# An adaLN-conditioned block: filling matmuls ahead of the first transposes, and another issue table

## The chip, the cores and the metric

The kernel runs on one core of a Trainium2 chip. Its engines work side by side, each through its own queue in strict order: TensorE (matmuls, PE in the profile), VectorE (DVE), ScalarE (ACT), GpSimd (POOL) and SyncE (SP), which issues most of the transfers between HBM and the on-chip memory. Matmul results land in PSUM, everything else lives in SBUF. The metric is the device time of one launch in microseconds. All inputs are bf16.

## The reference

```python
x = A_x                                            # 1 x 2048 x 512
sa, ca, ga, sb, cb, gb = split6(silu(c) @ w_mod)   # six rows of 512
h = layernorm(x) * (1 + ca) + sa
x = x + ga * A(h)
h = layernorm(x) * (1 + cb) + sb
x = x + gb * B(h)
```

`A` is an attention with 32 heads of 16 channels. A token looks at itself and at 7 earlier ones, two apart (window 8, dilation 2), with a softmax over these eight; `wqkv` (512 x 1536) goes in, `wo` (512 x 512) comes out. `B` normalises again, without scale and shift, and mixes over the tokens: `u = gelu(h^T @ w1 + b1)` with `w1` of 2048 x 1792, then `y = u @ w2 + b2` with `w2` of 1792 x 2048, transposed back.

## The kernel before

**Operations and the table.** The work is cut into 805 named operations. Each is added to a graph with what it reads and writes, the slot it takes or frees, and one or more ways to do it, each on another engine (`add`, `add_any`). A hand-written table, `ORDER`, names all of them once. `schedule()` walks it and issues each operation at its place; a mark behind the name picks the way: `:d` VectorE, `:a` ScalarE, `:p` POOL, `:s` nothing at all, `:q` a matmul in four pieces of 32 columns. Without a mark it is the first way. So the table fixes each engine's queue; what runs when follows from the waits between the queues. All engine instructions are issued through one wrapper, and so nearly every row of the profile has line 131: operations are told apart by tile and shape. Slots come from pools: six PSUM banks (psS), four large buffers (big), five vD buffers; a slot goes to the one that has been free longest.

**Tokens.** 2048 tokens are 16 tiles of 128 (`xx`, indices 0 to 15), in chunks of 2, 4, 4, 4 and 2 tiles. For each tile stand `ln1s`, `ln1v` (statistics, on VectorE, or on ScalarE as two passes into `junk`), for each chunk `rstd1`, `rste1`, `nb1` (inverse deviation and its product with the mean), and `n1` (normalise). Chunks 0 and 1 are transposed on TensorE (`tr0_0`, `tr1_0`, `tr1_2`), and the result is scaled by `a1col` as it is copied out (`hT0_k`, `hT1_k`); the later ones by DMA (`xt6` to `xt15`), with the scale multiplied into the weights (`wsc`).

**Modulation.** `cps` turns c into a column, `silu_exp` and `silu_dve` make silu(c), `modcols1` and `modcols0` multiply it with the first third of `w_mod` (loaded by `ld_wmod1`, `ld_wmod0`) in 16 one-column matmuls each. `a1col` is 1 + ca, `sab` is sa, from which `qvb0`, `qvb1` make the bias of q and v. The other four rows come later (`modrow`, `mrows`, `ld_row0` to `ld_row3`); the first is multiplied into `wo` (`woq_s`).

**Attention, chunk by chunk.** `qkv{ch}_{t}{j}` makes q (t=0), k (1) and v (2), `ev..` copies them out. `qk{ch}_0..3` multiplies q with eight shifted k on VectorE into a big buffer, `red` sums over channels on TensorE into `psL`. Then `max` (VectorE), `sub` (TensorE), `exp` (ScalarE), `esum` (TensorE), `rcp`, `rcq` (ScalarE), `smB` (VectorE); the weights and v are spread over partitions by DMA (`a2`, `vd`), `pv{ch}_0..3` multiplies them on VectorE, `pvacc` sums on TensorE, `oev` copies out, `wo{tile}` multiplies with woq, `x1_{tile}` writes the new x. After that `ln2..`, `n2`, `aff`, `afb`, `ln3..` and `h3` give the input of B.

**The MLP.** `mlp1_{i}_{ft}_{s}` adds token tiles from s on into the F-tile ft, in two or three passes over the tokens, whose parts are parked (`park`) and added (`padd`); then `gelu`. The slices of `w1` come through a ring of three buffers, wst0 to wst2 (`ld_w1_{i}_{f}`), which early on hold raw `wqkv`. `mlp2_{tile}` is the second product, `fin` the residual, `st_out` the store.

**Filling matmuls.** `WARM` is a list of eight counts. Block `warm0` (12 matmuls of 128 x 512, all of the identity with itself) is an operation of its own, tied in between `cps` and the `modcols` products by the key `wmA1`. The other seven may be done or skipped; the table skips six (`:s`) and has `warm1` (2 matmuls) as its last entry.

## Time and profile before

| what | us |
|---|---|
| median of three runs (lowest, highest) | 198.6 (197.77, 198.84) |
| span of the profiled execution | 196.8 |
| TensorE busy | 185.2 |
| VectorE busy | 156.6 |
| ScalarE busy | 124.9 |
| POOL busy | 19.9 |
| first transposes, `tr0_0`, start | 6.47 |
| `warm0`, start and length | 7.30, 5.20 |
| `modcols1`, start | 12.33 |
| first qkv product, start | 14.55 |
| first q·k product on VectorE, start | 18.07 |

The span runs from the first to the last instruction of one execution; the time of a run holds some 1.8 us more. Busy time is the time in which an engine has an instruction in it. Neighbouring matmuls overlap in the records, so the time from one start to the next says more about them than their own lengths. In a timeline row stand the start, the length, the engine, and behind the tiles how many instructions the row gathers; in brackets how long the engine was idle before it and what ended that.

### The profile page before, as it was taken

Reading aid. Unit: us, or ns where it says so; the run is one execution under the profiler, and the core shown is the slowest. Engines: PE = TensorE matmul, PEld = TensorE weight load, DVE = VectorE, ACT = ScalarE, POOL = GpSimd, SP = SyncE. Lnnn points to the kernel's source line nnn. Section 1 sums busy time; section 2 is a strip of 40 time slices with the busy share of each in tenths; the row PEclk is TensorE's granted clock in tenths of the full one; section 3 lists DMA queues with packets and bytes.
Section 4 is the critical chain, followed back from the end, with each engine's and each line's share of the span. In section 5 each row is a group of like instructions: output and inputs, shape, how many; then the busy total and the mean of one; then the engine's idle time right before and its main releaser. Section 6 shows DMA issues by size and latency. Waiting matters only on the chain.

```text
span 196.8 us, 4628 instructions
## 1 busy us (share of the span) xinstructions
PE 185.2 (94%) x1850; PEld 95.5 (48%) x1867; DVE 156.6 (80%) x244; ACT 124.9 (63%) x293; POOL 19.9 (10%) x38
## 2 busy tenths in 40 slices
PE   0699999999999999899999999999999999999994
PEld 0369554654444467244544454444444444444453
DVE  2888999999999999999999999965841633453664
ACT  6877999998999999999797889812760000000000
POOL 5123006320000005030000031200000000000000
PEclk9999999999999999999999999999999999999999
DMA  5998478778899732969674768888939293001112
GB/s 169 312 366 248 115 165 256 235 216 238 165 193 317 252 131 80 312 167 249 199 200 136 159 176 180 197 250 170 336 65 309 82 257 102 30 27 53 53 53 82
DMA packets 55369, 35.95 MB, mean 183 GB/s; under 512 B 24628, under 2 KB 52788, under 8 KB 55348
## 3 DMA queue, kind: packets, MB, share of 16 engines
q1 hardware_dynamic: 53468, 34.05, 63.2%
q10 hardware_dynamic: 1880, 1.61, 2.5%
q8 instruction: 14, 0.23, 0.5%
q14 instruction: 7, 0.06, 0.1%
HBM read 22.03 MB, written 2.10 MB: 123 GB/s over the span
## 4 chain that ended last, share of the span: by engine, by line
PE 73%; DVE 13%; ACT 5%; issue 3%; DMA 2%; SPq 1%; POOL 0%; DVEq 0%; ACTq 0%
PE psS L131 71%; DVE big L131 9%; DVE h L131 2%; PE psL L131 2%; ACT junk L131 1%; SPq L131 1%; DMA vD<-v_sb 1%; ACT xx L131 1%; DMA xx<-in_A_x_dram 1%; DVE m L131 1%; ACT o_sb L131 1%; ACT lsb L131 0%; DVE mv L131 0%; POOL h L131 0%; ACT v_sb L131 0%
## 5 line engine op out<-in xcount | busy, mean ns | idle before, releaser
L131 PEld LDWEIGHTS <-wst 128*128 128x128 bf16 (+1 forms) x566 | 35.5, 100 | 31.9 <-issue 1.3
L131 PE MATMUL psS<-h,wst 128*32 128x512 bf16 (+1 forms) x400 | 50.5, 379 | 0.4 <-issue 0.3
L131 DVE TENSOR_TENSOR big<-q_sb,k_f 128x4096 bf16<-128x4096 bf16 (+1 forms) x20 | 36.4, 1857 | 0.5 <-ACT k_f L131 0.5
L131 DVE TENSOR_TENSOR big<-a2sb,vD 128x4096 bf16<-128x4096 bf16 (+1 forms) x20 | 36.6, 1858 | 0.0
L131 DVE SCALAR_TENSOR_TENSOR h<-psS,bcol,rows_bc 128x512 f32<-128x512 f32 (+2 forms) x18 | 12.4, 690 | 24.2 <-PE psS L131 24.0
L131 PE MATMUL psS<-hT,w_qkv 128*32 128x512 bf16 (+3 forms) x414 | 28.7, 337 | 0.8 <-ACT v_sb L131 0.4
L131 PEld LDWEIGHTS <-w_qkv 128*32 128x32 bf16 (+1 forms) x462 | 19.9, 108 | 16.4 <-issue 2.7
L131 PE MATMUL psS<-gT,big 128*128 128x512 bf16 x109 | 24.3, 379 | 0.2
L131 POOL TENSOR_SCALAR h<-xx,rs,nb 128x512 bf16<-128x512 bf16 x6 | 10.6, 1777 | 84.2 <-DVE nb L131 84.2
L131 PEld LDWEIGHTS <-big 128*128 128x128 bf16 x144 | 12.0, 98 | 13.7 <-issue 0.5
L131 ACT ACTIVATE junk<-xx 128x512 bf16<-128x512 bf16 x28 | 17.7, 631 | 1.3 <-DVE xx L131 0.3
L131 ACT ACTIVATE h<-xx,nb,rs 128x512 bf16<-128x512 bf16 x22 | 17.2, 818 | 0.4 <-DVE nb L131 0.4
L131 PE MATMUL psS<-woq,o_sb 128*32 128x512 bf16 (+1 forms) x123 | 15.8, 380 | 0.4 <-ACT o_sb L131 0.4
L131 ACT ACTIVATE gT<-psS,bcol 128x512 bf16<-128x512 f32 x14 | 8.8, 686 | 10.6 <-DVE psS L131 10.6
L131 DVE TENSOR_TENSOR psS<-psS,gT 128x512 f32<-128x512 f32 x14 | 9.2, 695 | 6.3 <-PE psS L131 6.3
L131 DVE TENSOR_TENSOR h<-h,xx 128x512 bf16<-128x512 f32 (+2 forms) x18 | 11.4, 633 | 0.7
L131 ACT ACTIVATE q_sb<-psS,qvb 128x512 bf16<-128x512 f32 (+1 forms) x20 | 11.6, 603 | 0.3 <-PE psS L131 0.2
L131 PEld LDWEIGHTS <-group 128*32 128x32 bf16 x288 | 7.0, 96 | 9.8 <-issue 4.0
L131 PE MATMUL psS<-hT,wst 128*128 128x256 bf16 (+2 forms) x74 | 11.3, 333 | 0.1
L131 ACT ACTIVATE v_sb<-psS,qvb 128x512 bf16<-128x512 f32 (+1 forms) x20 | 11.2, 607 | 0.0
L131 DVE TENSOR_TENSOR h<-h,rows_bc 128x1024 bf16<-128x1024 bf16 (+2 forms) x14 | 10.5, 759 | 0.0
L131 ACT ACTIVATE k_f<-psS 128x512 bf16<-128x512 f32 x16 | 9.7, 606 | 1.1 <-PE psS L131 1.1
(90 smaller groups left out, 223.3 us busy)
## 6 DMA issues: line engine op xcount, KB each, us to landing
vD<-v_sb SPq DMA_DIRECT2D x12, 524.5 KB, 4.8
big<-in_B_w_dram SPq DMA_DIRECT2D x4, 896.0 KB, 7.5
vD<-v_sb SPq DMA_DIRECT2D x8, 268.5 KB, 3.1
wst<-in_B_w_dram SPq DMA_DIRECT2D x3, 640.0 KB, 5.4
xx<-in_A_x_dram SPq DMA_DIRECT2D x7, 256.0 KB, 5.6
wst<-in_B_w_dram SPq DMA_DIRECT2D x2, 800.0 KB, 4.7
gT<-in_w_mod_dram SPq DMA_DIRECT2D x3, 512.0 KB, 5.4
wst<-in_B_w_dram SPq DMA_DIRECT2D x2, 768.0 KB, 5.6
```

The costliest lines, as they stand in the source:

```text
L131: r = fn(*a, **k)
```

## The change

`warm0` becomes a block like the others: it may be placed anywhere, and the `modcols` products no longer depend on it. The counts become (5, 1, 5, 2, 2, 2, 1, 2). A second list, `GATE`, gives each block a token tile or none. A block with a tile multiplies the identity with that tile of `xx` instead of with itself, and so waits for that tile's load: `warm2` tile 1, `warm3` tile 8, `warm4` tile 2, `warm5` tile 4, `warm6` tile 6. Nobody reads what the fills write.

`ORDER` is another table with the same 805 names. All eight blocks, 20 matmuls, now stand ahead of `tr0_0`: `warm7`, `cps`, `warm1`, `warm0`, `warm4`, `warm3`, `warm5`, `warm6`, `warm2`. Behind `tr0_0` come `modcols1`, `tr1_2`, `tr1_0`, `modcols0`, `qkv0_00`, `qvb0`, `qkv0_10`, `qkv0_02`, `qkv0_12` (before: `warm0`, `modcols1`, `modcols0`, `tr1_2`, `tr1_0`, `qvb0`, `qkv0_00`, `qkv0_02`, `qkv0_10`, `qkv0_12`). Some 75 operations are done in another way: `n1_0` on ScalarE and `n1_1` on POOL instead of the other way round, more of `wsc` and of the normalisations on POOL, `x1_10` on VectorE (which spares `wo10` the matmul that adds the old x). Fewer products are cut in quarters: 1867 matmuls become 1737. Everywhere else too the operations stand in another order: `smB0` behind `rcq0` with `ev0_20` and `ev1_12` ahead of them on ScalarE, `woq_s` ahead of `qkv2_11`, `ld_w1_0_1152` and the loads behind it at other places.

```diff
@@ -178,60 +178,60 @@
 ORDER = """
-halo0 ident ld_c act_table cps silu_exp ld_x1 ld_x0 ln1s0 ln1v0 ln1s1:a ln1v1 rstd1_0 rste1_0 ld_x_2_8 ld_x_1_2 nb1_0
-consts ln1s9 silu_dve n1_1 n1_0:p tr0_0 ln1s8 ld_x_1_4 ln1s4:a ld_x_2_6 ln1s3:a warm0 ln1s5 ln1s7 ld_wmod1 ln1v5
-ld_wmod0 modcols1 modcols0 ln1v9 ln1v8 ln1v4 ln1s2 ln1v2 ld_wqkv0 ln1v7 ln1v3 ln1s6 ln1v6 rstd1_1 rste1_1 nb1_1 n1_4:d
-rstd1_2 rste1_2 n1_2:d n1_5:d nb1_2 ld_wqkv1 n1_3 n1_7 n1_6:d a1col hT0_2:d n1_9 tr1_2 tr1_0 hT1_1 wsc0_1:p hT0_1:d
-sab hT0_0:d ld_x_3_12 hT0_3:d hT1_3:d qvb0 qvb_cp0 qkv0_00 warm6:s wsc1_3:a hT1_2:d qkv0_02 ev0_00 ld_wqkv2 qkv0_10
-qkv0_12 ld_b2 ev0_10 ld_x_4_14 wsc1_2:p qkv0_20 wsc0_0 qvb1 ld_x_3_10 wsc0_3:p hT1_0:d ev0_02 wsc2_2:a ln1s13 ln1s12
-ev0_12 ln1v12 ln1v13 wsc1_1:a qkv0_22 qk0_1 qkv1_13 ld_wmod2 ld_wo3 qk0_0 qk0_2 n1_8 red0_0 red0_1 ln1s11:a qkv1_03:q
-qvb_cp1 qk0_3 xt6 red0_2 ld_wmod3 ev1_13 ev1_03 red0_3 mask wsc2_3:a ln1v11 ln1s10 ld_b1 ld_wo0 xt8 ev0_20 xt7 qkv1_11
-...
-n1_14 xt13 xt12 ln2q0 ln2q1 n1_15 qkv2_21 red2_1 red2_2 ln2w0 red2_3 xt11 rstd2_0 pv1_1 ev2_21 rste2_0 qkv3_10:q
-ev3_10 qkv3_02:q ev3_02 qkv3_00:q ev2_20 ev3_00 nb2_0 n2_1 n2_0 qkv3_11 max2 qkv3_01 ev3_01 sub2 pvacc1_1 oev1_1
-halo_v2 ld_row2 vd1_0 pvacc1_3 pv1_2 qkv3_12:q ld_row1 exp2 aff0 ev3_12 qkv3_13:q halo_v3:a ev3_11 pv1_0 esum2
-...
-fin6_0 mlp2_10_0 fin9_0 fin8_0 st_out8_0:a st_out6_0:a fin10_0 mlp2_7_0 fin7_0 st_out7_0:a mlp2_11_0 fin11_0 fin12_0
-st_out10_0:a st_out11_0:a st_out9_0 mlp2_14_0 fin14_0 st_out14_0 mlp2_13_0 fin13_0 st_out13_0:a mlp2_15_0 st_out12_0:a
-fin15_0 st_out15_0 mlp2_15_2 mlp2_15_1 fin15_2 fin15_1 st_out15_1 st_out15_2:a warm1
+ld_c ident warm7 act_table cps halo0 silu_exp silu_dve ld_x1 ln1s1 warm1 ln1v1 ld_x0 warm0 ld_x_2_8 ld_x_1_2 ln1s9:a
+ln1s0 consts warm4 ln1v0 rstd1_0 ln1s8 ld_x_1_4 ln1s3 ln1s5 ln1s2 ln1v9 warm3 ld_x_2_6 warm5 ln1v5 ln1v3 ln1v8
+ld_wmod1 ln1v2 rste1_0 ln1s4:a ln1v4 rstd1_1 rste1_1 warm6 nb1_0 ld_wmod0 n1_1:p warm2 ln1s7 n1_0 nb1_1 n1_4:p ln1s6
+n1_3:d n1_2:d ln1v7 ln1v6 tr0_0 rstd1_2 rste1_2 ld_wqkv0 n1_5:d modcols1 tr1_2 tr1_0 a1col ld_wqkv1 wsc1_0:p modcols0
+ld_x_3_12 hT0_2 nb1_2 hT0_0:d n1_6:d hT0_3:d hT1_2:d wsc0_1 hT0_1 sab hT1_3 ld_wqkv2 qkv0_00 ld_b2 wsc1_2:p wsc0_3:a
+hT1_0:d wsc0_2:a qvb0 ld_x_4_14 n1_8:d wsc0_0:a qvb_cp0 n1_7:d qkv0_10 ln1s13 ld_x_3_10 qkv0_02 ev0_00 ld_wmod2 ln1s12
+ev0_10 qkv0_12 hT1_1 qk0_1 ev0_02 qkv0_20 qk0_0 ld_wo3 ev0_12 ln1s15:a qkv0_22 qkv1_03 qkv1_13 red0_0 n1_9 ev1_03
+ln1v13 red0_1 qk0_2 ev1_13 qk0_3 red0_2 xt6 qkv1_11:q red0_3 mask qkv1_01 qvb1 ln1s10:a ln1s11 qk1_3 wsc1_1:a ev1_11
+...
+qkv2_02:q rcq1 ev2_11 ev2_01 oev0_2 pvacc0_1 oev0_0 nb1_4 n1_15:p ev2_02 smB1 qk2_1 xt10 ev2_13 red2_0 biascols
+qkv2_12 n1_14 vd1_3 qkv2_23 ev2_12 wo0 wo1 vd1_2 qk2_3 x1_0 ln2q0 x1_1 halo_v2 qkv2_20 xt11 qkv2_22 a2_1_0 biascols_cp
+qkv2_21 qk2_2 red2_1 a2_1_1 a2_1_2 a2_1_3 ev2_22 ln2m0 red2_2 ev2_20 ln2q1 xt13 xt12 pv1_2 ln2w0 red2_3 rstd2_0 ev2_23
+vd1_0 xt14 qkv3_00:q vd1_1 ld_row1 ev2_21 rste2_0 pv1_3 qkv3_12:q nb2_0 xt15 max2 pvacc1_2 qkv3_02 ev3_12 qkv3_01
+pv1_0 ld_row3 ev3_00 sub2 qkv3_10 oev1_2 n2_0 ev3_01 qkv3_03 n2_1 ev3_10 exp2 aff0 pvacc1_0 qkv3_11:q ev3_03 oev1_0
+pv1_1 ev3_11 esum2:q rcp2 halo_v3:a vd2_0 ev3_02 pvacc1_3 oev1_3 vd2_2 qkv3_20:q vd2_1 ev3_20 pvacc1_1 qkv3_13 qk3_0
+afb0 rcq2 smB2 a2_2_1 qkv3_23 oev1_1 ev3_13 wo3 wo5 ln3s1:a qk3_1 qk3_2 ev3_23 ln3s0:a x1_5 qkv3_22 x1_3 wo2 x1_2
+ln2q3 qk3_3 a2_2_0 wo4 x1_4 qkv4_00 ln2q4 red3_0 red3_1 qkv4_12:q a2_2_3 vd2_3 ln2q5 ln2q2 ev4_12 ln2m2 ev3_22 red3_2
+...
+mlp2_8_0 fin8_0 st_out5_0:a mlp2_10_0 st_out11_0:a st_out8_0:a st_out6_0 mlp2_14_0 fin9_0 st_out9_0:a mlp2_13_0
+fin10_0 st_out10_0:a fin14_0 st_out14_0:a mlp2_12_0 fin13_0 fin12_0 mlp2_15_0 st_out13_0 st_out12_0:a fin15_0
+mlp2_15_2 fin15_2 st_out15_0:a st_out15_2:a mlp2_15_1 fin15_1 st_out15_1:a
 """
@@ -264,7 +264,8 @@
     GRP=(2, 4, 4, 2, 1),
     XDMA=(2, 3, 4),
     INJ=(),
-    WARM=(12, 2, 2, 2, 2, 2, 2, 2),
+    WARM=(5, 1, 5, 2, 2, 2, 1, 2),
+    GATE=(None, None, 1, 8, 2, 4, 6, None),
 ):
     nc = _OrderedNC(tc, 1)
     G = _Graph(dict(ps=6, big=NBIG, vd=NVD))
@@ -522,20 +523,18 @@
 
     for w_, n_w in enumerate(WARM):
         s_w = _Slot("ps")
-
-        def f_warm(s_w=s_w, n_w=n_w):
+        g_w = GATE[w_]
+
+        def f_warm(s_w=s_w, n_w=n_w, g_w=g_w):
+            rhs = _ap(ident[:, 0:1], [[0, 4], [1, P]]) if g_w is None else xx[:, g_w, :]
             for _ in range(n_w):
-                nc.tensor.matmul(ps(s_w), lhsT=ident[:], rhs=_ap(ident[:, 0:1], [[0, 4], [1, P]]), start=True, stop=True)
-        if w_ == 0:
-            f_warm0, s_w0 = f_warm, s_w
-            continue
-        G.add_any([("pe", 0.216 * n_w, f_warm), ("skip", 0.0, lambda: None)], reads=["ident"], alloc=s_w, frees=s_w,
-                  name=f"warm{w_}")
+                nc.tensor.matmul(ps(s_w), lhsT=ident[:], rhs=rhs, start=True, stop=True)
+        G.add_any([("pe", 0.216 * n_w, f_warm), ("skip", 0.0, lambda: None)],
+                  reads=["ident"] + ([] if g_w is None else [("xx", g_w)]), alloc=s_w, frees=s_w, name=f"warm{w_}")
 
     s_c, s_m = _Slot("ps"), (_Slot("ps"), _Slot("ps"))
     add("pe", 0.18, lambda: nc.tensor.matmul(ps(s_c)[:, 0:KT], lhsT=c_t[:], rhs=ident[0:KT, 0:KT], start=True,
                                              stop=True), reads=["c_t", "ident"], alloc=s_c, name="cps")
-    add("pe", 0.216 * WARM[0], f_warm0, after=[G.ops[-1]], alloc=s_w0, frees=s_w0, writes=["wmA1"], name="warm0")
     add("act", 0.2, lambda: nc.scalar.activation(ecol[:], ps(s_c)[:, 0:KT], ACT.Exp, scale=-1.0), reads=[s_c, "act_table"],
         writes=["ecol"], name="silu_exp")
 
@@ -550,10 +549,10 @@
             for kt in range(KT):
                 nc.tensor.matmul(ps(s_m[v])[:, dt_:dt_ + 1], lhsT=wmodA[:, kt, v * D + dt_ * P: v * D + (dt_ + 1) * P],
                                  rhs=sc[:, kt:kt + 1], start=(kt == 0), stop=(kt == KT - 1))
-    add("pe", 0.42, lambda: f_cols(1), reads=["sc", ("wmodA", 1), "wmA1"], writes=["wmA1"], alloc=s_m[1], name="modcols1")
+    add("pe", 0.42, lambda: f_cols(1), reads=["sc", ("wmodA", 1)], alloc=s_m[1], name="modcols1")
     add("dve", 0.15, lambda: nc.vector.tensor_scalar_add(a1col[:], ps(s_m[1])[:, 0:KT], 1.0), frees=s_m[1],
         writes=["a1col"], name="a1col")
-    add("pe", 0.42, lambda: f_cols(0), reads=["sc", ("wmodA", 0), "wmA1"], frees=s_wm, alloc=s_m[0], name="modcols0")
+    add("pe", 0.42, lambda: f_cols(0), reads=["sc", ("wmodA", 0)], frees=s_wm, alloc=s_m[0], name="modcols0")
     add("dve", 0.15, lambda: nc.vector.tensor_copy(sab[:], ps(s_m[0])[:, 0:KT]), frees=s_m[0], writes=["sab"],
         name="sab")
     scale_w(1)
```

## The prediction

> **What bounds the kernel now.** I read the busy shares first, then the busy time by stretch, then the chain, then the early timelines.

> ```profile
> PE 185.2 (94%) x1850; PEld 95.5 (48%) x1867; DVE 156.6 (80%) x244; ACT 124.9 (63%) x293; POOL 19.9 (10%) x38
> PEclk9999999999999999999999999999999999999999
> ...
> 18.07:101.89 83.82, 81.75 (x1178) 43.61 (x1184) 83.65 (x82) 80.51 (x192) 10.62 (x5) 1.00 0.74 200
> ...
> 120.00:140.00 20.00, 19.95 (x93) 9.05 (x93) 15.30 (x35) 11.01 (x25) 1.78 (x2) 1.00 0.82 206
> ```

> The columns of a stretch are its length, then PE, PEld, DVE, ACT, POOL. TensorE looks like the bound with 94%, but that is an average of three stages. From 18.07 us (first q·k product) to 101.89 us VectorE works 83.65 of 83.82 us: it has no idle time left to remove. TensorE shows 81.75 there, and ScalarE 80.51. Behind that only TensorE is full (19.95 of 20). Ahead of 18 us neither is.

> ```profile
> 0.81 2.16 DMA xx<-in_A_x_dram
> 5.64 0.78 POOL h L131
> 6.47 10.88 PE psS L131 x108
> 18.07 1.79 DVE big L131 x2
> ...
> 96.00 5.86 PE psS L131 x136
> 101.89 0.62 PE psS L131 x8
> 102.67 16.71 PE psS L131 x182
> 119.54 10.74 PE psS L131 x49
> ...
> 101.76 1.22 DVE L131 TENSOR_TENSOR h<-h,rows_bc 128x2048 bf16<-128x2048 bf16 x1
> ```

> The first eight rows are the chain of waits (start, length, what). It goes through TensorE up to qkv0, hands over to VectorE at 18.07, and wanders between saturated engines. At 101.89 the last eight-matmul piece is `pvacc3_3`, which starts as VectorE leaves `pv3_3` for the next operation (last row, VectorE's timeline): there TensorE waits for VectorE. From then on it is matmuls back to back, 49 in 10.74 us, so 0.219 us each. So the time is: start of `qk0_1`, plus VectorE's queue up to `pv3_3`, plus TensorE's queue behind it.

> ```profile
> 2.20 0.18 PE L131 MATMUL psS<-ident,c_t 4*128 4x4 bf16 x1 [2.20 <-DMA c_t<-in_c_dram]
> 6.47 1.03 PE L131 MATMUL psS<-ident,h 128*128 128x128 bf16 x8 [4.09 <-POOL h L131]
> 7.30 5.20 PE L131 MATMUL psS<-ident 128*128 128x512 bf16 x12
> 12.33 0.94 PE L131 MATMUL psS<-sc,big 128*128 128x1 bf16 x32
> 14.55 3.66 PE L131 MATMUL psS<-hT,wst 128*128 128x256 bf16 x32
> ...
> 5.57 0.81 ACT L131 ACTIVATE h<-xx,nb,rs 128x512 bf16<-128x512 bf16 x1 [0.23 <-DVE nb L131]
> 17.38 0.60 ACT L131 ACTIVATE k_f<-psS 128x512 bf16<-128x512 f32 x1 [0.91 <-PE psS L131]
> ...
> 3.73 1.02 SPq L131 DMA_DIRECT2D big<-in_w_mod_dram  x2
> 4.80 1.55 SPq L131 DMA_DIRECT2D wst<-in_A_wqkv_dram  x2
> ...
> big<-in_w_mod_dram SPq DMA_DIRECT2D x2, 512.0 KB, 6.0
> wst<-in_A_wqkv_dram SPq DMA_DIRECT2D x2, 512.0 KB, 8.3
> ```

> The twelve fills of `warm0` take 5.20 us, 0.43 each, twice the later 0.219: TensorE is cold. They hold `modcols1` until 12.33, while its weights, issued at 3.73, land 6.0 us later, at 9.7. The fills cost 2.6 us of waiting there.

> **The change, part by part.** Fills: 12 become 20, all ahead of `tr0_0`. Eight read only the identity and run from the `cps` product (2.20) on, cold: 8 × 0.43 = 3.4 us, to about 5.5. Twelve read xx tiles and wait for their loads. The token loads leave in the order of before, the last pair by

> ```profile
> 6.66 0.63 ACT L131 ACTIVATE junk<-xx 128x512 bf16<-128x512 bf16 x1 [0.28 <-DMA xx<-in_A_x_dram]
> 3.50 0.69 DVE L131 BATCH_NORM_STATS2 st<-xx 128x6 f32<-128x512 bf16 x1 [3.50 <-DMA xx<-in_A_x_dram]
> ```

> VectorE gets tile 0 at 3.50 and ScalarE the pair 4, 5 at 6.66; the pair 6, 7, issued next, I put at 8.0 (estimate: one more 256 KB at the stretch's 200 to 300 GB/s). So fills end at 9.4 with the clock open, 10.6 if all is cold.

> First transposes: in the new table VectorE works through more statistics (`ln1s8 s3 s5 s2`, 0.69 each) ahead of `nb1_0`, and ScalarE's `ln1s4` (two passes, 1.5 us from 6.66) sits in front of them; I get `nb1_0` near 9.0, `n1_0` on ScalarE (0.81) and `n1_1` on POOL near 9.9, `tr0_0` near 10.3 instead of 6.47. That costs nothing by itself, since `modcols1` can't start ahead of 9.7. `modcols1` comes at 10.7 to 11.5 instead of 12.33, and `a1col` 0.6 us later, but behind `n1_5:d` on VectorE. `qkv0_00` needs w_q, the first load of the 4.80 row (with its 8.3 us not behind 13.1), and hT0 tiles that are shared out between ScalarE and VectorE: I get 13.5 instead of 14.55. Then the gain shrinks:

> ```profile
> 14.20 2.05 POOL L131 TENSOR_SCALAR w_qkv<-wst,a1col 128x512 bf16<-128x512 bf16 x3 [0.35 <-DMA wst<-in_A_wqkv_dram]
> ```

> The second load, w_k, holds POOL until 14.20 and gates `qkv0_10` as well; that one also stands behind `sab` and `qvb0` in TensorE's queue, and `ev0_10` (17.38 before, 0.60) then waits for its turn on ScalarE. For `qk0_1` I take 17.5 instead of 18.07: −0.6, bounds −1.0 and −0.1.

> VectorE's queue from `qk0_1` to `pv3_3`: both tables hold the same 24 full products at 2.28, 12 half ones at 1.22 and, but for five items, the same rest. After drops `ln1s10` (0.69) and `h3_3:d` (0.40) from it and adds `ln1s11` (0.69) and two variances (0.17 each): −0.1. This is the argument's core: without idle time in the stretch, nothing that ScalarE, POOL or TensorE save (ScalarE loses 3.7 us of work over the kernel, POOL gains 6) can shorten it; new waits can lengthen it.

> ```profile
> L131 DVE TENSOR_TENSOR big<-a2sb,vD 128x4096 bf16<-128x4096 bf16 x12 | 27.3, 2286 | 0.0
> L131 DVE TENSOR_TENSOR big<-q_sb,k_f 128x4096 bf16<-128x4096 bf16 x12 | 27.1, 2284 | 0.0
> L131 DVE TENSOR_TENSOR big<-q_sb,k_f 128x2048 bf16<-128x2048 bf16 x8 | 9.4, 1217 | 0.5 <-ACT k_f L131 0.5
> ...
> 31.42 4.91 POOL L131 TENSOR_SCALAR h<-xx,rs,nb 128x512 bf16<-128x512 bf16 x1 [15.17 <-DVE nb L131]
> 37.78 0.63 SPq L131 DMA_DIRECT2D woq<-in_A_wo_dram  x1
> 38.59 2.37 SPq L131 DMA_TRANSPOSE hT<-h  x1
> ```

> New waits on VectorE, by walking both queues with the rows' durations: `smB0` behind a later `rcq0` (ScalarE now has `ev0_20` and `ev1_12` in between): +0.3; `qk1_2` behind `ev1_02`, which follows `rcq0`: +0.2; `qk2_0` behind `ev2_10`, now right ahead of it: +0.4. `woq_s` moves from behind sixteen-odd items to about 41 us; it reads row 0 and all four loads of woq, the last of which leaves SP at 37.78 in before and lands some 2 us later: 0 to +0.9, I take 0.2, since most of these loads move forward on SP too. Together +1.1, bounds 0 and +2.6. Part is taken back, as VectorE behind a wait finds its later inputs ready: `sub0` and `sub1` stand earlier on TensorE by 0.8 and 0.4 us of its queue. I take back 0.3 (0 to 0.6).

> POOL: it takes `n1_10`, `n1_15`, `n2_3` and more wsc pieces. In the VectorE stretch such a pass took 4.91 us where 0.78 is usual, while the products beside it kept their 2.28: POOL pays, not VectorE. Its readers (`xt10`, the qkv3 block) stand some 8 us behind: nothing; without that cover up to 4.

> TensorE: 1867 matmuls become 1737, mostly because 32-column quads became whole matmuls; columns rise by six fills (eight more, minus the last two that went; net 6 × 0.219, all ahead of 10 us). Of its order only the part behind `pvacc3_3` counts; by columns it is 90.9 us in both. There `wo10` loses its residual matmul (−0.2) and other work moved by as much.

> Weight ring: between the last reader of a slot and the first of its next load the new table leaves 25 matmuls (5.5 us) where before had 30 and 31 (6.6, 6.8). The loads need

> ```profile
> wst<-in_B_w_dram SPq DMA_DIRECT2D x3, 640.0 KB, 5.4
> wst<-in_B_w_dram SPq DMA_DIRECT2D x2, 800.0 KB, 4.7
> wst<-in_B_w_dram SPq DMA_DIRECT2D x2, 768.0 KB, 5.6
> ```

> 4.7 to 5.6, with 0.6 for SP's issue ahead: 0 to +0.8 each at two places; I take +0.2 in all. The last normalised tiles: `mlp1_1_0_10` asks for `h3_10` about 1 us earlier in both queues than before (margin there 1 us), and h3_12 and h3_14 go to POOL: 0 to +1.0, I take 0.1.

> Tail: the last stores all leave on ScalarE's queue: ±0.1, taken 0. `warm1` ends no chain before: 0.

> Sum: −0.6 −0.1 +1.1 −0.3 +0.2 +0.1 = +0.4. The profiled execution had a span of 196.8; the median of the runs is 198.6, 1.8 more around it. So 197.2 in the span and **199.0 us**.

> **Rivals.** (a) *TensorE is the bound in the middle and gets shorter.* The timeline shows untiled and tiled matmuls in turn:

> ```profile
> 32.52 2.09 PE L131 MATMUL psL<-big,group 128*32 128x512 bf16 x32
> 34.43 1.05 PE L131 MATMUL psS<-hT,w_qkv 128*32 128x512 bf16 x16
> ...
> 50.41 1.05 PE L131 MATMUL psS<-hT,w_qkv 128*128 128x512 bf16 x4
> 51.40 1.48 PE L131 MATMUL psL<-big,group 128*32 128x512 bf16 x24
> ```

> From 32.52 to 34.43 pass 1.91 us for 32 quarter matmuls, which are eight whole ones, 8 × 0.219 = 1.75; from 50.41 to 51.40 0.99 for four, 0.88. So a switch loses 0.11 to 0.16 us. The new order has 16 switches instead of 26: if TensorE sets the pace, 1.1 to 1.6 us go, and with the 0.6 of the start and no new wait it is 198.6 − 2.0 = 196.6; I put it at 196.4 to 197.3. Against it: VectorE has no idle time for that. [...] (b) *The cold clock stays.* The gated fills leave gaps where loads are late, and qkv0 starts at 0.43 instead of 0.22 us per 512 columns. If it warms up halfway through, its 3.66 us grow by 1.8, of which some 0.4 is lost in waits for ScalarE that are there anyway: 200.4. It decides once `qkv0_00` runs cold. Here the granted clock in the page reads 9 from the start, so only the durations tell. [...] (c) *Late queue wait.* One ring load or `woq_s` misses by its upper bound, or `h3_10` does: +1.0 to +2 on top: 200.5. (d) *The start doesn't move*, because w_k and `qvb0`, not the fills, gate `qk0_1`: 199.4, inside my forecast's own range.

> **How the numbers follow.** Two runs of one kernel differ by about 0.5% (1.0 us), so that is the line between change and none. Forecast with (d): 0.45, own range 198.0 to 200.1, above 199.6 in two fifths of it and below 197.6 hardly ever. (a) 0.25, all faster. (b) 0.10 and (c) 0.20, slower. Faster 0.27, same 0.27, slower 0.46. Leaving out a tenth at each end: 196.8 to 201.0.

> **What would show it.** Fills ahead of `tr0_0`, which starts near 10.3; `modcols1` near 11; `qk0_1` at 17.1 to 18; `sab` ahead of it. Small VectorE waits on ScalarE near 30, 31 and 36 us where before had none; the `pvacc3_3` piece near 102.2; behind it 0.219 per matmul without a gap above 0.3. I am wrong if VectorE's busy time from `qk0_1` to `pv3_3` is below 83 us, if qkv0 runs at 0.2 us per matmul, or if TensorE waits for wst or h3 behind 102 us.

## The result, and the profile after

The changed kernel takes 198.92 us (median of 20 runs, 198.12 to 200.38), the one before 198.34 (median of 20, 197.77 to 199.2). The ratio is 1.0036, 95% interval 1.0021 to 1.0052: slower by a third of a per cent, which is within the line of 0.5% between change and none. The forecast was 199.0. All ratios in this document are taken against runs of the kernel before from the same set, without the two runs that lay over 1.5% above the fastest of their kernel (one of before, 201.43, and one of e9, 202.49); they need not be the quotient of the two medians.

The profiled executions don't show it: both have a span of 196.8 us. Busy time, and two stretches of the kernel after (length, PE, PEld, DVE, ACT, POOL):

```profile
PE 187.4 (95%) x1737; PEld 95.9 (49%) x1737; DVE 158.3 (80%) x246; ACT 122.4 (62%) x289; POOL 33.7 (17%) x44
...
16.82:101.28 84.46, 81.76 (x1076) 44.08 (x1074) 84.45 (x83) 79.30 (x186) 23.36 (x10) 1.00 0.70 197
...
120.00:140.00 20.00, 20.00 (x94) 9.05 (x93) 15.69 (x40) 12.34 (x31) 3.07 (x4) 1.00 0.91 243
```

The first product starts at 16.82 instead of 18.07, and `pv3_3` ends at 101.28 instead of 101.84. Between them VectorE has no idle time at all, but the stretch takes 84.46 us where it took 83.77 (83.60 of them busy). The chain of waits shows the same two ends:

```profile
16.82 1.76 DVE big L131 x2
...
101.34 92.02 PE psS L131 x540
```

TensorE still starts `pvacc3_3` when VectorE leaves `pv3_3`, and is full from there on. The last matmul of the second product ends 0.47 us earlier than before (193.34, 193.80; the two fills of `warm1` behind it are gone), and so does VectorE's last operation; these are the last VectorE rows of before, then of after:

```profile
194.23 0.29 DVE L131 TENSOR_TENSOR h<-h,xx 128x128 bf16<-128x128 f32 x1
```

```profile
193.76 0.29 DVE L131 TENSOR_TENSOR h<-h,xx 128x128 bf16<-128x128 f32 x1
```

Behind them SyncE has seen the last store land at 196.0 and 195.6; then the engines' closing exchange takes 0.8 us before and 1.2 after, and the spans come out equal. Early on, TensorE in the kernel after:

```profile
2.52 2.74 PE L131 MATMUL psS<-ident 128*128 128x512 bf16 x6
5.40 1.73 PE L131 MATMUL psS<-xx,ident 128*128 128x512 bf16 x6
7.33 1.47 PE L131 MATMUL psS<-xx,ident 128*128 128x512 bf16 x6 [0.20 <-DMA xx<-in_A_x_dram]
9.48 0.62 PE L131 MATMUL psS<-ident,h 128*128 128x128 bf16 x8 [0.68 <-ACT h L131]
10.01 0.55 PE L131 MATMUL psS<-sc,big 128*128 128x1 bf16 x16
12.90 1.15 PE L131 MATMUL psS<-hT,wst 128*128 128x256 bf16 x8 [0.61 <-DMA wst<-in_A_wqkv_dram]
```

The first fills take 0.43 us each, those from 6 us on 0.22: the clock is open by then (the clock records of the trace begin at 5.98; in the kernel before they begin at 12.23, near the end of `warm0`). The modulation product comes at 10.01 instead of 12.33, the first qkv product at 12.90 instead of 14.55.

What the profile can't show is the scatter. Of the 20 runs 16 lie between 198.12 and 199.24, and four between 199.97 and 200.38; before had no run above 199.2 in these (in a later set of 23 it had three at 199.9 to 201.4, in the other three sets none above 199.48). Each run also gives TensorE's mean granted clock. Two of the four upper runs have 0.991, the other two 1.0 and 0.997. The upper runs are not all of the 0.58 us between the medians: without them the median is 198.71, still 0.37 above before. So there are two questions: what took back the 1.25 us of the start, and what makes the upper runs.

### The profile page after: what moved, and what is told of

Its sections match the earlier page's. It is cut to its first block, busy times and chain, and to the rows that moved or that the text cites. A ratio compares the mean times of both kernels' runs of the same rounds, so it can differ in the third digit from the quotient of the medians.

```text
span 196.8 us, 4384 instructions
## 1 busy us (share of the span) xinstructions
PE 187.4 (95%) x1737; PEld 95.9 (49%) x1737; DVE 158.3 (80%) x246; ACT 122.4 (62%) x289; POOL 33.7 (17%) x44
## 4 chain that ended last, share of the span: by engine, by line
PE 50%; DVE 27%; issue 8%; ACT 6%; DMA 4%; SPq 3%; ACTq 0%; DVEq 0%
PE psS L131 50%; DVE big L131 16%; DMA wst<-in_B_w_dram 3%; DVE st L131 3%; SPq L131 3%; DVE h L131 2%; DVE m L131 2%; ACT h L131 1%; DVE mv L131 1%; DVE lsb L131 1%; ACT w_qkv L131 1%; ACT hT L131 1%; ACT L131 1%; DMA a2sb<-lsb 1%; ACT o_sb L131 1%
## 5 line engine op out<-in xcount | busy, mean ns | idle before, releaser
L131 PEld LDWEIGHTS <-wst 128*128 128x128 bf16 (+1 forms) x560 | 36.2, 100 | 32.3 <-issue 1.3
L131 PE MATMUL psS<-h,wst 128*32 128x512 bf16 (+1 forms) x398 | 50.9, 379 | 0.0
L131 DVE TENSOR_TENSOR big<-q_sb,k_f 128x4096 bf16<-128x4096 bf16 (+1 forms) x20 | 37.7, 1912 | 0.3 <-ACT k_f L131 0.3
L131 DVE TENSOR_TENSOR big<-a2sb,vD 128x4096 bf16<-128x4096 bf16 (+1 forms) x20 | 36.8, 1856 | 0.0
L131 DVE SCALAR_TENSOR_TENSOR h<-psS,bcol,rows_bc 128x512 f32<-128x512 f32 (+2 forms) x18 | 12.4, 690 | 22.0 <-PE psS L131 21.8
L131 PE MATMUL psS<-hT,w_qkv 128*32 128x256 bf16 (+3 forms) x360 | 29.1, 330 | 0.0
L131 PEld LDWEIGHTS <-w_qkv 128*32 128x32 bf16 (+1 forms) x402 | 20.2, 108 | 15.4 <-issue 0.8
L131 POOL TENSOR_SCALAR h<-xx,rs,nb 128x512 bf16<-128x512 bf16 x8 | 15.1, 1889 | 72.8 <-PE psS L131 56.6
L131 PE MATMUL psS<-gT,big 128*128 128x512 bf16 x112 | 24.8, 379 | 0.0
L131 PEld LDWEIGHTS <-big 128*128 128x128 bf16 x144 | 11.9, 97 | 13.3
L131 ACT ACTIVATE junk<-xx 128x512 bf16<-128x512 bf16 x26 | 16.4, 631 | 2.7 <-DMA xx<-in_A_x_dram 1.8
L131 PE MATMUL psS<-woq,o_sb 128*128 128x512 bf16 x64 | 15.9, 379 | 0.0
L131 ACT ACTIVATE gT<-psS,bcol 128x512 bf16<-128x512 f32 x14 | 9.0, 686 | 8.7 <-DVE psS L131 8.7
L131 DVE TENSOR_TENSOR psS<-psS,gT 128x512 f32<-128x512 f32 x14 | 9.4, 697 | 5.4 <-PE psS L131 5.4
L131 DVE TENSOR_TENSOR h<-h,xx 128x512 bf16<-128x512 f32 (+2 forms) x18 | 11.4, 633 | 2.9 <-DMA out_dram<-h 2.2
L131 PEld LDWEIGHTS <-group 128*32 128x32 bf16 x288 | 6.9, 96 | 11.2 <-DVE big L131 4.7
L131 PE MATMUL psS<-hT,wst 128*128 128x256 bf16 (+2 forms) x76 | 11.7, 335 | 0.6 <-DMA wst<-in_A_wqkv_dram 0.6
L131 ACT ACTIVATE h<-xx,nb,rs 128x512 bf16<-128x512 bf16 x15 | 12.0, 817 | 0.3 <-DVE nb L131 0.2
L131 PE MATMUL psS<-big,group 128*32 128x512 bf16 (+1 forms) x160 | 10.2, 338 | 1.9 <-DVE big L131 1.9
L131 ACT ACTIVATE v_sb<-psS,qvb 128x512 bf16<-128x512 f32 (+1 forms) x20 | 11.3, 603 | 0.8 <-issue 0.8
L131 ACT ACTIVATE q_sb<-psS,qvb 128x512 bf16<-128x512 f32 (+1 forms) x20 | 11.7, 607 | 0.0
L131 DVE TENSOR_TENSOR h<-h,rows_bc 128x1024 bf16<-128x1024 bf16 (+2 forms) x14 | 10.7, 762 | 0.1
## 6 DMA issues: line engine op xcount, KB each, us to landing
gT<-in_w_mod_dram SPq DMA_DIRECT2D x3, 512.0 KB, 4.3
wst<-in_B_w_dram SPq DMA_DIRECT2D x2, 768.0 KB, 5.0
```

The lines of the kernel that those rows point to most:

```text
L131: r = fn(*a, **k)
```

## The experiments

**e1: the new table with the old fills.** Twelve fills between the first transposes and `modcols1`, and the two of `warm1` as the last entry; the other six blocks are skipped.

```diff
-    WARM=(5, 1, 5, 2, 2, 2, 1, 2),
-    GATE=(None, None, 1, 8, 2, 4, 6, None),
+    WARM=(12, 2, 2, 2, 2, 2, 2, 2),
+    GATE=(None,) * 8,
...
-n1_3:d n1_2:d ln1v7 ln1v6 tr0_0 rstd1_2
+n1_3:d n1_2:d ln1v7 ln1v6 tr0_0 warm0 rstd1_2
```

> The new table, but with the twelve fills of before between the first transposes and the modulation product, and no other block. Theory S (the new fills give the earlier start, the rest of the table gives it back): the first q.k product starts 0.5 to 1.3 us later than in the new kernel's 16.82, and the time rises to 199.3 to 200.0. Rival P (the start comes from the order of the normalisations, the fills don't matter): start within 0.3 of 16.82 and time within 0.4 of the new kernel. On the scatter: the new kernel has runs at 198.1 to 199.3 and others at 200.0 to 200.4; if the gated fills make the second group (theory C, the clock of TensorE closes in a gap), it is absent here; if the table makes it (rival Q, a late wait), it stays.

Measured: 202.85 us, ratio 1.0222 (1.0202 to 1.0243), first product at 21.96.

```profile
9.83 1.03 PE L131 MATMUL psS<-ident,h 128*128 128x128 bf16 x8 [7.44 <-ACT h L131]
10.66 4.60 PE L131 MATMUL psS<-ident 128*128 128x512 bf16 x12
15.09 0.54 PE L131 MATMUL psS<-sc,big 128*128 128x1 bf16 x16
```

In the new table the first transposes are ready only at 9.8, and twelve mostly cold fills behind them (the clock records begin at 14.38) hold the modulation product until 15.09. The start is 5.1 us later; the time grows by 3.9. Theory S had the direction, but a quarter of the size. None of the five runs stands above the others, which is too few to say anything of the upper runs. At this place the new table can't take the fills; whether it needs them elsewhere is the next run's question.

**e8: the new kernel without any fill.** All eight blocks are skipped (`:s`).

> The new kernel with all eight blocks left out. Theory S: TensorE is cold until the qkv products have run for one window; qkv0 takes up to 7 us instead of 3.7, the first product of VectorE starts 1.5 to 2.5 us later: 200.2 to 201.2. Rival P (fills don't matter, the order does): within 0.4 of the new kernel.

Measured: 198.93, ratio 1.0041 (1.0013 to 1.0068): the time of the changed kernel, whose ratio was 1.0036. The fills buy nothing.

```profile
9.64 1.03 PE L131 MATMUL psS<-ident,h 128*128 128x128 bf16 x8 [7.14 <-ACT h L131]
10.94 1.87 PE L131 MATMUL psS<-ident,h 128*128 128x128 bf16 x16
13.07 1.89 PE L131 MATMUL psS<-hT,wst 128*128 128x256 bf16 x8
15.32 2.79 PE L131 MATMUL psS<-hT,wst 128*128 128x256 bf16 x24
```

Without them the transposes and the first eight qkv products run cold (1.89 against 1.15 us), but the clock opens ahead of the other 24: its records begin at 15.26, 5.6 us behind the first transpose and 2.2 behind the first qkv product. (From the start of TensorE's first row of several matmuls to the first clock record it is 4.5 us in after, 4.6 in e1 and 5.8 in before.) No run shows that one window of qkv products opens the clock; qkv0 takes 5.0 us from its first row to the end of its last, not up to 7. The first product starts at 17.15, 0.3 later than in the profile of the changed kernel, but other profiles with the same fills and the same table up to there have 16.86 (e3), 17.02 (e11) and 17.24 (e9). So the early start comes from the rest of the new table (rival P), which also takes `warm0` away from ahead of `modcols1`, and not from the new fills. What the old table would do without any fill was not run. Three of the twelve runs are upper ones (199.47 to 201.23), all with a clock of 0.996 or more: they need no closed clock.

**e2: the old table with the new fills**, ahead of `tr0_0`, which is moved behind `ld_x_2_6`.

```diff
-consts ln1s9 silu_dve n1_1 n1_0:p tr0_0 ln1s8 ld_x_1_4 ln1s4:a ld_x_2_6 ln1s3:a warm0 ln1s5
+consts ln1s9 silu_dve n1_1 n1_0:p ln1s8 ld_x_1_4 ln1s4:a ld_x_2_6 warm4 warm3 warm5 warm6 warm2 tr0_0 ln1s3:a ln1s5
```

> The old table, but with the twenty fills of the new one ahead of the first transposes, which no longer hold the modulation product. Theory S: the first q.k product starts 0.5 to 1.2 us ahead of 18.07, and as the old table has hardly any POOL work there, VectorE keeps that: 197.3 to 198.0. Rival P: start within 0.3 of before, time within 0.4 of before. Theory C: some runs stand 1 to 2 us above the others. Rival Q: none do.

Measured: 199.62, ratio 1.0066 (1.0042 to 1.0091), first product at 18.86, later than before. All six runs have a mean clock of 0.989 to 0.991. The clock by stretches (it stands two columns ahead of the rate in GB/s):

```profile
9.60:13.00 3.40, 1.99 (x49) 1.62 (x47) 3.08 (x14) 2.77 (x8) 0.00 (x0) 1.00 1.09 381
13.00:16.40 3.40, 3.40 (x37) 2.84 (x35) 3.22 (x12) 2.48 (x5) 2.12 (x3) 0.50 1.10 348
16.40:20.00 3.60, 3.60 (x41) 3.56 (x39) 1.94 (x4) 2.54 (x7) 0.76 (x2) 1.00 0.79 236
```

From 13.0 to 16.4 the granted clock is 0.50, just when the qkv products run: 32 of them take 4.65 us instead of 3.66. In the 3.4 us before, TensorE was busy for 1.99, 32 of the 49 matmuls being one column wide. Half the clock for 3.4 of 197 us is 0.9% of the mean, which is the 0.991 of the runs. So theory S and rival P both fail, and the closing that theory C expected in some runs came in all six. The run doesn't tell whether the old table would keep an earlier start: without the 1.0 us that the closed clock costs in qkv0, the first product would stand near 17.9 (estimate), 0.2 ahead of before.

**e4: the new kernel, fills ungated** (`GATE=(None,) * 8`).

> The new kernel with all twenty fills on the identity, so that none waits for a load. Theory C: the fills end 0.3 to 0.7 us earlier, the gap ahead of the first transposes grows from 0.7 to above 1 us, and the share of runs near 200 changes. Rival Q: the share stays, and the time stays within 0.3 of the new kernel, since the first transposes wait for ScalarE's normalisation anyway.

Measured: 198.98, ratio 1.0027 (0.9998 to 1.0056). The fills end at 8.7, only 0.1 earlier than in the changed kernel, and the gap ahead of the transposes is 1.07 us. Six of twelve runs have a clock of 0.983 to 0.991, three of these lie at 199.7 to 200.8; in the changed kernel it was three of twenty, two of them upper runs. The six have a mean of 199.6 us, the other six of 198.7. The profile fell on one of the six:

```profile
13.80:17.10 3.30, 3.30 (x31) 2.51 (x30) 2.18 (x6) 2.73 (x6) 2.78 (x4) 0.50 1.10 347
```

The first product starts at 17.81 there, 1.0 later than in the profile of the changed kernel. So a closed clock makes a part of the upper runs (theory C), and by these counts the gates make it rarer.

**e6: bridging fills.** Three more ahead of `tr0_0`, three between `modcols0` and the first qkv product.

```diff
-    WARM=(5, 1, 5, 2, 2, 2, 1, 2),
-    GATE=(None, None, 1, 8, 2, 4, 6, None),
+    WARM=(5, 1, 8, 2, 2, 2, 1, 2, 3),
+    GATE=(None, None, 1, 8, 2, 4, 6, None, None),
...
-ld_wqkv2 qkv0_00 ld_b2
+ld_wqkv2 warm8 qkv0_00 ld_b2
```

> The new kernel with three more fills ahead of the first transposes and three between modcols0 and the first qkv product, where TensorE waits for loads anyway. Theory C (the clock closes in runs in which a window of about 3.4 us falls on one-column products and gaps, as in the profiles of e2 and e4, where it stood at 0.50 from 13 to 16.4 and from 13.8 to 17): no run above 199.7, median 198.3 to 198.7. Rival: the upper runs have another cause, a quarter of them stays near 200.

Measured: 198.74, ratio 1.0013 (0.9990 to 1.0036). No run has a clock below 0.995. In the four kernels with these fills (e6, e7, e10, e12) that makes none of 42 runs; in the five with the gated fills and no bridge (after, e3, e5, e9, e11) it was six of 62. The first product starts at 17.24 in its profile, 0.4 later than in that of the changed kernel; e9, without the bridge, has 17.24 too, so that is no price of the bridge. One upper run is left, 200.43, with a clock of 1.0, and the profile fell on it. VectorE and SP in e6:

```profile
40.00 1.22 DVE L131 TENSOR_TENSOR woq<-woq,rows_bc 128x2048 bf16<-128x2048 bf16 x1
42.98 1.23 DVE L131 TENSOR_TENSOR big<-a2sb,vD 128x2048 bf16<-128x2048 bf16 x1 [1.76 <-DMA vD<-v_sb]
...
37.60 0.60 SPq L131 DMA_DIRECT2D vD<-v_sb  x1
```

`pv0_1` waits 1.76 us for `vd0_1`, the spread of v. The new table puts this transfer behind three others on SP, at 37.59; in the profile of after it lands at 40.61, 0.5 us ahead of its product (41.15); here ten of its sixteen parts are in by 40.53, as there, but the last six come at 42.80 to 42.86. What held them is not shown. The old table issues its last spread of the chunk at 35.31, landing at 37.82, with more than a microsecond to spare.

**e11: `vd0_1` alone issued earlier, behind `vd0_0`.**

```diff
-halo_v1 vd0_2 vd0_0 ld_row0 ld_wo2
+halo_v1 vd0_2 vd0_0 vd0_1 ld_row0 ld_wo2
...
-woq_s qkv2_11:q vd0_1 pvacc0_3
+woq_s qkv2_11:q pvacc0_3
```

> The new kernel with vd0_1 alone issued earlier, behind vd0_0; the other two spreads stay where they are, since in e10 the extra one at 42.47 pushed the four a2 transfers of chunk 1 back by 1.6 us and pv1 waited 1.21. Theory L for this one margin: no run above 199.7 except by a closed clock (mean below 0.995), median 198.6 to 198.8. Rival: the upper runs come from later transfers of the same queue (a2_1, vd1_0), and a fifth or more stays near 200.

Measured: 198.72, ratio 1.0018 (0.9998 to 1.0038). One run of twelve is above 199.5 (200.02), and its clock is 0.991. Upper runs (above 199.45) with a clock of 0.996 or more were 11 of 92 in after and e3 to e8; in e11 and e12, where this transfer is early, none of 24, which by luck alone would come once in fifteen to twenty such trials. The 24 are also one set on one chip, on which the kernel before stayed below 199.4 as well. And this transfer isn't the only cause: the kernel before, with its wide margin, has three such runs in 112 (199.48, 199.91, 200.60). The mechanism is shown in one profile, its share only by these counts.

**e9 and e10: three spreads earlier.** e9 also moves `vd1_0` behind `vd1_2` and `vd2_3` behind `vd2_1`; e10 does this on top of e7 (below).

> The new kernel with three of its spreads of v issued earlier on SP: vd0_1 behind vd0_0, vd1_0 behind vd1_2, vd2_3 behind vd2_1. In the new kernel's profile they land 0.5, 0.4 and 0.9 us ahead of the product that reads them; in the profile of e6, which fell on an upper run, vd0_1 landed at 42.86 instead of 40.61 and its product waited 1.76 us. Theory L (these narrow margins make the upper runs): no run above 199.7, median 0.2 to 0.4 below the new kernel's 198.92. Theory C (the clock makes them): a fifth of the runs stays near 200, and the median within 0.2.

> e7 (bridging fills, scalings and n1_15 off POOL) with the three early spreads of e9. Theories C, L and V together: no run above 199.3, median 197.8 to 198.2, faster than before by 0.1 to 0.3%. If the gains don't add: 198.2 to 198.6.

Measured: e9 200.77, ratio 1.0083 (1.0046 to 1.0119), five of six runs above 200.5; e10 199.86, ratio 1.0059 (1.0037 to 1.0081). Both theories missed. VectorE in e10:

```profile
51.35 2.29 DVE L131 TENSOR_TENSOR big<-a2sb,vD 128x4096 bf16<-128x4096 bf16 x1 [1.21 <-DMA a2sb<-lsb]
```

The additional spread stands on SP ahead of the four `a2` transfers of chunk 1; the first of them leaves at 45.98 instead of 44.38, and the product waits 1.21 us. In this stretch SP's queue has no room: what is moved forward pushes back what is needed next. For e9 that is inferred from e10: its profile fell on its one low run (198.76), where the first `a2` leaves at 45.45 and VectorE doesn't wait for it.

**e3: two scalings of w_v from POOL to ScalarE.** The other question: VectorE's 0.69 us. Rows of POOL and VectorE in the kernel after:

```profile
16.71 3.38 POOL L131 TENSOR_SCALAR w_qkv<-h,a1col 128x512 bf16<-128x512 bf16 x2
...
16.82 2.79 DVE L131 TENSOR_TENSOR big<-q_sb,k_f 128x2048 bf16<-128x2048 bf16 x2 [0.27 <-ACT k_f L131]
19.63 1.54 DVE L131 TENSOR_TENSOR big<-q_sb,k_f 128x2048 bf16<-128x2048 bf16 x1
```

Two half products take 2.36 us elsewhere; here 2.79, and the third 1.54 instead of 1.22. A third long one is `qk2_2` at 47.36, 2.70 instead of 2.28, with POOL's `n1_15` running until 47.92. Together 1.17 us. The rows around `qk2_2` in the kernel after, then VectorE's in e7 (below), where `n1_15` isn't on POOL:

```profile
42.55 5.38 POOL L131 TENSOR_SCALAR h<-xx,rs,nb 128x512 bf16<-128x512 bf16 x1 [6.34 <-DVE nb L131]
...
42.96 7.11 DVE L131 TENSOR_TENSOR big<-q_sb,k_f 128x4096 bf16<-128x4096 bf16 x3
```

```profile
43.07 6.70 DVE L131 TENSOR_TENSOR big<-q_sb,k_f 128x4096 bf16<-128x4096 bf16 x3
```

The length of a POOL row doesn't tell which product pays: `n1_15` is on record beside all three products of its row, and only the last one is long.

```diff
-qk1_0 qkv1_23 wsc2_2:p ld_wo1 smB0
+qk1_0 qkv1_23 ld_wo1 smB0
...
-n1_13 wsc2_0:p a2_0_1
+n1_13 a2_0_1
...
-pvacc0_1 oev0_0 nb1_4
+pvacc0_1 oev0_0 wsc2_2:a wsc2_0:a nb1_4
```

> The new kernel with two scalings of w_v taken from POOL and given to ScalarE, later. Theory V (a pass of POOL that is under way when a product starts holds VectorE's product up): the first and the third product, 1.65 and 1.54 us in the new kernel, take 1.22 again, VectorE's queue is 0.7 us ahead behind them, and the time falls by 0.4 to 0.7. Rival: the long products have another cause (their reads, the DMAs): they stay above 1.4 us and the time stays within 0.3.

Measured: 198.8, ratio 1.0030 (1.0003 to 1.0056). VectorE in e3:

```profile
16.86 2.36 DVE L131 TENSOR_TENSOR big<-q_sb,k_f 128x2048 bf16<-128x2048 bf16 x2
19.23 2.33 DVE L131 TENSOR_TENSOR big<-q_sb,k_f 128x2048 bf16<-128x2048 bf16 x2
...
45.56 2.29 DVE L131 TENSOR_TENSOR big<-q_sb,k_f 128x4096 bf16<-128x4096 bf16 x1 [1.06 <-ACT k_f L131]
```

The cause is shown: without POOL's two passes the first four products take their usual time, and VectorE is 0.75 us ahead. (`qk2_2` is 2.28 here too; `n1_15` ends at 45.06, in VectorE's wait ahead of 45.56.) But the two passes, now on ScalarE, stand ahead of chunk 2's copies, and VectorE waits 1.06 us for them at 45.56: the time is not better.

**e5: the same two passes at other places on ScalarE** (`wsc2_2:a` ahead of `rstd1_3`, `wsc2_0:a` ahead of `rcp1`).

> As e3, but one of the two scalings goes into ScalarE's gap of 0.79 us at 26 us and the other ahead of the softmax's rcp1, since in e3 both stood in front of the copy of q for qk2_3, which then waited 1.06 us. Theory V: products of 1.22 us as in e3, VectorE's queue from the first product to the last pv3 some 0.4 to 0.7 us shorter than 84.45, time 198.1 to 198.5. Rival W (VectorE gains nothing by being early, since another queue sets the pace in the middle): a new wait of VectorE takes the 0.7 us back elsewhere, and the time stays within 0.3 of the new kernel.

Measured: 198.97, ratio 1.0034 (1.0011 to 1.0056). The first products take 1.22, but `qk1_0` now waits 0.34 us for ScalarE, the first product starts at 17.11, and now `qk2_3` is the long one beside `n1_15` (2.69): the queue takes 84.24. Rival W, a new wait elsewhere, holds here.

**e7: e5 and e6 together, and `n1_15` from POOL to ScalarE**, behind `ev2_12`.

> e5 and e6 together, and n1_15 from POOL to ScalarE, so that no product of VectorE is held up by POOL. Theories V and C: both gains add, 197.4 to 198.1, faster than before. Rival W: 198.3 to 198.8.

Measured: 198.19, ratio 1.0001 (0.9976 to 1.0027). No product is longer than 2.3, and VectorE's queue takes 83.78, as before. 0.1 to 0.8 slower than expected by V and C, faster than W. In the same set it is 0.55 us ahead of e6, which has the bridge but keeps the passes on POOL.

**e12: e7 with `vd0_1` behind `vd0_0`.**

> e7 with vd0_1 behind vd0_0. If the upper runs of e7 (199.54 and 200.34 of twelve) came from that margin, none is left and the median is 198.0 to 198.2, faster than before by 0.1 to 0.25%. Otherwise as e7: 198.2 with one run in six above 199.5.

Measured: 197.98 us (twelve runs, 197.77 to 198.63), ratio to before 0.9973 (0.9958 to 0.9989): faster than before, as expected, and without an upper run. Its stretch from the first product to `pv3_3`:

```profile
17.38:101.15 83.77, 81.67 (x1076) 43.80 (x1073) 83.43 (x83) 80.74 (x189) 10.27 (x7) 1.00 0.71 194
```

POOL is busy for 10.27 us of it instead of 23.36, and VectorE needs 83.77 instead of 84.45, idle 0.34 of it. Its start is 0.69 us ahead of before, its queue takes the same time as there, and its median is 0.53 us ahead of before in the same set. The changed kernel's median, in another set, is 0.94 us higher than that of e12; e11, the changed kernel with this one transfer early, is 0.74 higher in the same set.

## Why the prediction was right, step by step

The time was met within 0.1 us, and much of that is luck: several terms were wrong and cancelled, and the median of before that the sum started from (198.6, three runs) lay 0.26 above the one measured beside the result (198.34).

| step | forecast | profiled executions |
|---|---|---|
| start of `qk0_1` | −0.6 (−1.0 to −0.1) | −1.25 |
| VectorE's queue: fewer operations | −0.1 | −0.3 |
| VectorE's queue: new waits, less what is taken back | +0.8 | none |
| VectorE's queue: POOL beside the products | 0 | +1.17 |
| VectorE's queue in all | +0.7 | +0.69 |
| TensorE behind `pvacc3_3` | +0.3 | +0.1 |
| tail | 0 (±0.1) | +0.4 |
| sum | +0.4 | −0.06; in the medians +0.58 |

**What held.** The frame did: start, VectorE's queue, TensorE's queue behind it. VectorE is full in the middle, so the earlier start could reach the end only as far as this queue allowed, and TensorE's savings could not.

**The start.** The step "`qkv0_00` ... I get 13.5" failed: it came at 12.90, and the first product lay outside my bounds. The expected late `ev0_10` wasn't late. e8, without fills, still starts at 17.15, so the fills have little or no part in it.

**The new waits.** The waits at `smB0`, `qk1_2`, `qk2_0` and `woq_s` didn't come in the profiled execution: VectorE's busy time fills its whole stretch. So the largest term of the sum failed, and the queue's +0.69 met its forecast of +0.7 for another reason. The sum over two queues' rows put ScalarE's copies too late. (From one start to the next, the dropped and added operations make about −0.3: `h3_3` −0.32, the statistics −0.12, two more variances +0.16. What is still missing between −0.3 + 1.17 and +0.69 is about the idle time that before had, 0.17 in its stretch.) One wait of this kind does come in some runs, but at a place that I hadn't priced (`vd0_1`, 1.76 us in e6).

**POOL.** "POOL pays, not VectorE" failed. I had read it from a POOL pass of 4.91 us beside products that kept their 2.28; there POOL waited through the products. In the kernel after VectorE pays three times: 1.65 us for a product of 1.22, with the pass running from 16.71 to 17.40 and the product from 16.82, and likewise at 19.63 and 47.36. The three long products are those in which a pass ends, 0.5 to 0.6 us behind the product's start; other products, at 18.40, 42.96 and 45.16, begin with a pass on record too and keep their time. So it reads as if a pass on record either waits, or does its 0.7 us of work and makes VectorE wait; when POOL gets its turn is not shown. The trace shows a loss on both sides: the product at 16.82 lost 0.43 us to a pass that had 0.58 to run, and POOL's next pass took 2.71 us instead of 0.69.

**The rivals.** (a) fell: ten switches fewer, and TensorE still waits for `pv3_3`. (b) came true in part, in 3 of 20 runs (two of them upper ones), and by another course, as far as the profiles of e2 and e4 show it: the clock opened at 6 to 7 us and closed again for 3.4 us in qkv0. No profile of the changed kernel fell on such a run. In the 3.4 us ahead of the closing in e2 TensorE was busy for 1.99 us, and its longest gap was 0.88. The low chance that I gave (b), 0.10, had no run behind it: the only closing in the profile of before is at its end (from 196.55). (c) came true too, in some runs, with the spread of v in place of the weight ring, `woq_s` or `h3_10`. So the median, unlike the profile, is above before: 0.06 us less in the profiled pair, but these two lie 0.3 above the median of before and 0.3 below the median of after. How the four upper runs share out between the two causes is settled only for the two with a clock of 0.991, and of the 0.37 us by which the other sixteen lie above before no run gives a full account. The profiled execution starts `qk0_1` earlier than those of e3, e9 and e11, by up to 0.4 us, and e11's run of 198.91, near the median, has the same long products (1.58, 1.53, 2.70) and a queue of 84.43; e7 and e12 show that taking the passes off POOL, with the bridge, wins that much back.

(d), that the start doesn't move, fell. By the sum's own terms it would have been 199.6, not 199.4; and with the forecast's shares slower adds up to 0.48 and same to 0.25, not 0.46 and 0.27.

## What to carry to other kernels

An engine without idle time (here VectorE, busy for 84.45 of 84.46 us) gets nothing from the savings of its neighbours; look instead at what can lengthen its own instructions, and here that was work moved to POOL, which made three of VectorE's products 0.3 to 0.4 us longer. When one profile shows no difference and the medians do, look at the scatter of runs: transfers that land half a microsecond ahead of their reader (a wait of 1.76 us in the profile of e6), and a clock that may close (0.50 for 3.4 us in e2 and e4), cost in some runs only. A transfer moved forward in a full queue delays the one behind it (1.6 us in e10), so move one at a time. And test a filling matmul by leaving it out: here the time was the same without all twenty (ratios 1.0041 and 1.0036).

## What was not expected of the hardware

```profile
10.40:13.80 3.40, 2.67 (x52) 2.14 (x50) 2.97 (x14) 1.77 (x5) 0.00 (x0) 0.99 1.10 367
```

```profile
9.50:12.90 3.40, 2.68 (x56) 2.26 (x57) 2.97 (x13) 1.17 (x4) 0.54 (x1) 1.00 1.08 377
```

```profile
8.55:11.97 3.42, 2.50 (x43) 1.84 (x42) 2.99 (x11) 1.91 (x6) 1.54 (x2) 1.00 1.07 367
```

The columns that the matmuls stream fit better. Take each profile in windows of 3.413 us (the closings in e2 and e4 last 3.4, and the clock record from the opening to the closing at the end is 184.320 us long in before and 191.146 in after, 54 and 56 times 3.413) from the opening of its clock, and add up the widths of the matmuls that start in each, where a matmul in a quarter of the array counts a quarter. The windows ahead of the closings in e2 and e4 have 1696 and 3101 columns, those at the end of the kernels at most 2176. The thinnest windows that closed nothing have 3104 (after, e3, e5), 3360 (e9) and 3601 (e11), and with the bridge 4100 or more. So the kernel after stands at the edge, which would explain why it closes in some runs only, and why three fills of 512 columns in the gap were enough. That is an ordering of fourteen profiles with a near tie in it (3101 and 3104), no test.

Also, the page's granted clock reads 9 in the first microseconds, in which a fill takes 0.43 us instead of 0.22: the row shows a closing, but not that the clock hasn't opened yet. The clock records behind it begin only when it opens, at 12.23 us in before and 5.98 in after.
